# Score, solve and near copies in other shapes, constants inside the written order, and a new order, in a fused RWKV-7 and SwiGLU kernel

## The chip, the cores and the metric

The kernel runs on one core of a Trainium2 chip. The metric is the device time of one execution in microseconds; where several runs of a kernel are given, their median is compared.

## The reference

Two blocks follow each other. The first is the RWKV-7 recurrence over 768 steps for 4 x 8 heads of width 40; the second is a SwiGLU feed-forward block with RMS norm over 3072 tokens, 320 wide, with 1536 hidden units. All is float32.

```python
# r, k, v, w, a, b: (4, 8, 768, 40); state: (4, 8, 40, 40), zero at first
for t in range(S):
    y[:, :, t] = np.einsum('bhd,bhde->bhe', rt, state)
    Sa = np.einsum('bhde,bhe->bhd', state, at)
    state_decay = state * wt[:, :, None, :] - np.einsum('bhd,bhe->bhde', Sa, bt)
    state = state_decay + np.einsum('bhd,bhe->bhde', vt, kt)
x = y.transpose(0, 2, 1, 3).reshape(3072, 320)
xn = x / np.sqrt(np.mean(x * x, axis=-1, keepdims=True) + 1e-06) * rms_g
g = xn @ w_gate
out = (g * (1.0 / (1.0 + np.exp(-g))) * (xn @ w_val)) @ w_out
```

## The kernel before, in words

The sequence is cut into 24 chunks of 32 steps. Inside a chunk the recurrence becomes matrix products: a 32 x 32 triangular system per head is solved, and only the state passes from chunk to chunk. Batch and head give 32 sequences; they lie as 16 groups along the free axis (index n for 8 heads, o for two of the batches) and as four blocks of 32 partitions (i and q).

A chunk has three pieces of code. `front(c)` loads w, a, k, b and v, transposes them on TensorE (`turned`, line 527 in the profile), and builds by five levels (distances 1, 2, 4, 8, 16) the products of decayed k, b and a. The tile `LT` receives them: three predicated copies with the mask `near` (distances 1 to 3 inside groups of four steps) and one with `msk` for each higher level. `inverse(c)` takes the part of `LT` that belongs to b, sends it through DRAM (`sB`) into `M`, where each partition holds one sequence's matrix, eliminates row by row on VectorE (`Yi`, `tmp`), and sends the result through DRAM (`sY`) into the tile `LI`. While c is below `BLOCKED` (5) the elimination works on two 16 x 16 blocks, and `main` then solves twice with a correction by `LB` between. `main(c)` forms the right-hand side (the products called state and lower), multiplies it by the inverse (solve), updates the state, makes the scores of r against k and v (score), masks them by level (`As`, with `msi`), multiplies them with the level's k and b (level) and collects y. After the norm it writes the chunk, transposed, into `xg`.

`feed(g)` is the feed-forward block for a group of one or two chunks: products of `xg` with the resident weights `wf` into PSUM, silu on ScalarE (`sg`), product on VectorE (`hT`), and the product with w_out accumulated in `po`. `narrow(f, h, ...)` turns the weights, which arrive as 64-bit floats, into float32 on VectorE and ScalarE during the first chunks. The feed products wait for nothing but `xg`, `sg` and `hT`, and fill TensorE between the dependent steps of the chunks.

No scheduler decides the order at run time. Every operation is recorded by helpers as a piece of a `Plan`: `dve` (line 478, with `tt`, `ts`, `where` and `dcopy` above it), `act`, `copy` and `scale` for ScalarE (501, 505, 508), `ptt`, `pcopy` and `blank` for GpSimd (511, 514, 517), `dma` (521), and `pe` with `mm` (524) and `flip` (527). Therefore nearly all instructions carry one of these line numbers, and tiles tell them apart. `Plan.issue` then emits the pieces in the total order written in the table `ORDER`; `PAIRS` gives each PSUM use one of three double banks. Every engine and every DMA queue works through its own instructions in that order, so an instruction that waits holds up all behind it on its engine. SP issues most transfers, POOL (GpSimd's queue) the loads of w, a, k, b and v after the first chunk. `Turns(n, ...)` is a ring of n buffers; those with a `zero` view are cleared once by `blank`. The constants ahead of that (`ident`, `eye`, `msk`, `near`, `msi`) are issued directly, ahead of everything in the order.

The lines of the change in the kernel before, where the product of the score covers both batches i at once and the solve takes two 32 x 32 blocks as one block-diagonal 64 x 64 matrix:

```python
solve = [mm(U[half(i), o, col(m)], LI[half(i), 4 * o + m], Xs[half(i), o, col(m)])
         for m in range(4) for i in range(2) for o in range(2)]                      # 843
pe("score", [mm(sc[:, o, n], vut[part(o), n], R["rE"][part(o), n, :, tk])
             for n in range(N) for o in range(2)])                                   # 884
```

`half(i)` is the partitions 64i to 64i+63, `part(o)` the first 40 of a half, and `rows(i, x)` a block of 32.

Of the kernel before, what the change touches and what calls it, by code (L numbers as in the profile page):

```python
# [397 lines left out]
def kernel(  # L398
# [130 lines left out]
    def pe(kind, steps, more=[]):  # L529
        def issue(at):  # L530
            return [s[3](at) for s in steps]
        plan.add("PE", 0.0, 0.0, issue, [s[0] for s in steps] + more, [x for s in steps for x in s[1:3]],
                 kind=kind, many=sum(s[4] for s in steps))


    ident = const.tile([P, P], FP32, name="ident")
    nc.gpsimd.memset(ident, 0.0)
    nc.gpsimd.affine_select(ident, ident, pattern=[[-1, P]], channel_multiplier=1, base=0,
                            compare_op=ALU.not_equal, fill=1.0)
# [532 lines left out]
```

## Time and profile before

| | |
|---|---|
| median of 3 runs | 1184.49 us (1182.04 to 1191.2) |
| profiled execution, its time | 1190.31 us |
| its span, first to last instruction | 1188.5 us |
| TensorE busy, matmul | 1041.0 us (88%), 22896 records |
| TensorE busy, weight loads | 840.1 us (71%) |
| VectorE busy | 891.3 us (75%), 2917 instructions |
| ScalarE busy | 445.4 us (37%) |
| GpSimd busy | 304.6 us (26%) |
| mean granted TensorE clock | 0.929 |
| DMA traffic | 68.67 MB, mean 58 GB/s |

An fp32 product leaves two matmul records and two weight loads; a transpose leaves one of each. Matmuls overlap, so the mean time of one is a latency, and the busy time of a group divided by its count is what one occupies. Rows by shape read: line, engine, operation, output <- inputs, for a product weights K*M and then moving K x N, count, busy us, mean ns of one, then the engine's idle time just before and what ended it. PE is TensorE's matmuls, PEld its weight loads, DVE VectorE, ACT ScalarE, POOL GpSimd.

### The profile page before, as it was taken

Reading aid. Unit: us, or ns where it says so; the run is one execution under the profiler, and the core shown is the slowest. Engines: PE = TensorE matmul, PEld = TensorE weight load, DVE = VectorE, ACT = ScalarE, POOL = GpSimd, SP = SyncE. Lnnn points to the kernel's source line nnn. Section 1 sums busy time; section 2 is a strip of 40 time slices with the busy share of each in tenths; the row PEclk is TensorE's granted clock in tenths of the full one; section 3 lists DMA queues with packets and bytes.
Section 4 is the critical chain, followed back from the end, with each engine's and each line's share of the span. In section 5 each row is a group of like instructions: output and inputs, shape, how many; then the busy total and the mean of one; then the engine's idle time right before and its main releaser. Section 6 shows DMA issues by size and latency. Waiting matters only on the chain.

```text
span 1188.5 us, 52214 instructions
## 1 busy us (share of the span) xinstructions
PE 1041.0 (88%) x22896; PEld 840.1 (71%) x22896; DVE 891.3 (75%) x2917; ACT 445.4 (37%) x945; POOL 304.6 (26%) x534
## 2 busy tenths in 40 slices
PE   1528788998989899899899899999999999999998
PEld 1527777877877777777677777677777787777777
DVE  6999867669678777687787787797697686877541
ACT  4765552433242342433333433433324323413211
POOL 8203313223123232124124113124213132320000
PEclk9998667999998999998989999998899897999799
DMA  5464432231231231222223223222322222221110
GB/s 134 116 174 107 97 67 45 47 62 36 56 69 31 52 64 36 53 41 62 46 49 65 55 38 59 55 45 59 63 38 52 46 56 50 44 42 33 30 20 18
DMA packets 147043, 68.67 MB, mean 58 GB/s; under 512 B 121088, under 2 KB 136384, under 8 KB 146816
## 3 DMA queue, kind: packets, MB, share of 16 engines
q1 hardware_dynamic: 128448, 42.37, 16.0%
q0 software_dynamic: 16192, 22.64, 10.0%
q8 instruction: 180, 2.95, 1.0%
q10 hardware_dynamic: 2176, 0.33, 0.2%
q14 instruction: 47, 0.39, 0.1%
HBM read 55.05 MB, written 10.22 MB: 55 GB/s over the span
## 4 chain that ended last, share of the span: by engine, by line
PE 52%; DVE 28%; DMA 6%; issue 6%; SPq 3%; POOL 2%; ACT 2%; DVEq 0%; ACTq 0%; POOLq 0%
PE ps L524 39%; PE po L524 9%; DVE LT L478 7%; PE ps L527 4%; SPq L521 3%; DVE K L478 3%; DVE y L478 3%; DVE Yi L478 3%; DVE tmp L478 3%; DVE As L478 1%; DVE Ab L478 1%; DVE wf L478 1%; DMA sB<-LT 1%; DMA M<-sB 1%; POOL kbn L521 1%
## 5 line engine op out<-in xcount | busy, mean ns | idle before, releaser
L524 PE MATMUL ps<-xg,wf 64*128 64x256 f32 (+3 forms) x1872 | 391.8, 397 | 6.5 <-DVE LT L478 2.9
L524 PEld LDWEIGHTS ps<-xg,wf 64*128 64x128 f32 (+1 forms) x1872 | 281.7, 201 | 64.6 <-issue 20.7
L524 PE MATMUL po<-wf,hT 128*128 128x320 f32 x576 | 191.1, 465 | 0.6 <-DVE hT L478 0.6
L478 DVE TENSOR_TENSOR tmp<-Yi,M 128x60 f32<-128x60 f32 (+26 forms) x664 | 138.8, 209 | 38.9 <-ACT Yi L505 15.1
L478 DVE TENSOR_TENSOR Yi<-Yi,tmp 128x60 f32<-128x60 f32 (+26 forms) x664 | 138.0, 208 | 12.9
L524 PE MATMUL ps<-Ab,K 40*64 40x56 f32 x4608 | 101.8, 251 | 50.3 <-DVE K L478 12.8
L524 PEld LDWEIGHTS ps<-Ab,K 40*64 40x64 f32 x4608 | 93.3, 163 | 65.9 <-issue 33.5
L524 PEld LDWEIGHTS po<-wf,hT 128*128 128x128 f32 x576 | 106.9, 198 | 37.3 <-issue 3.8
L501 ACT ACTIVATE sg<-ps 128x256 f32<-128x256 f32 (+1 forms) x156 | 55.1, 368 | 173.1 <-PE ps L524 169.8
L478 DVE TENSOR_TENSOR hT<-ps,sg 128x256 f32<-128x256 f32 (+1 forms) x156 | 61.0, 401 | 65.9 <-PE ps L524 36.4
L478 DVE TENSOR_TENSOR As<-ps,msi 128x256 f32<-128x256 f32 (+1 forms) x192 | 85.9, 484 | 29.3 <-PE ps L524 29.3
L505 ACT COPY KN<-ps 128x640 f32<-128x640 f32 x96 | 66.0, 692 | 111.1 <-PE ps L527 49.1
L478 DVE TENSOR_TENSOR K<-K,T 128x512 f32<-128x512 f32 (+1 forms) x192 | 95.8, 511 | 3.4 <-PE ps L527 1.1
L521 POOL DMA_DIRECT2D wn<-in_w_dram x92 | 51.9, 567 | 177.2 <-DVE KN L478 128.1
L478 DVE COPY_PREDICATED LT<-near,ps 128x384 f32<-128x384 uint32 (+2 forms) x72 | 93.5, 1298 | 4.6 <-PE ps L524 4.1
L521 POOL DMA_DIRECT2D kbn<-in_b_dram x92 | 53.8, 587 | 165.6 <-PE ps L524 164.0
L521 POOL DMA_DIRECT2D kbn<-in_k_dram x92 | 53.7, 587 | 133.5 <-PE ps L524 127.9
L505 ACT COPY K<-K 128x512 f32<-128x512 f32 x96 | 60.9, 634 | 64.1 <-DVE K L478 33.7
L521 POOL DMA_DIRECT2D VU<-in_v_dram x92 | 53.8, 586 | 101.3 <-PE ps L524 98.7
L524 PE MATMUL ps<-As,KN 128*40 128x32 f32 x3072 | 74.9, 209 | 3.8 <-DVE As L478 2.5
L524 PEld LDWEIGHTS ps<-As,KN 128*40 128x40 f32 x3072 | 69.1, 130 | 11.2 <-DVE As L478 4.2
L511 POOL TENSOR_TENSOR ss<-ss,mhalf 128x1 f32<-128x1 f32 x24 | 14.8, 615 | 217.9 <-DVE ss L478 193.5
(131 smaller groups left out, 1507.1 us busy)
## 6 DMA issues: line engine op xcount, KB each, us to landing
M<-sB SPq DMA_DIRECT2D x96, 128.0 KB, 2.9
wan<-in_r_dram SPq DMA_DIRECT2D x24, 160.0 KB, 3.6
kbn<-in_b_dram POOLq DMA_DIRECT2D x92, 40.0 KB, 2.2
kbn<-in_k_dram POOLq DMA_DIRECT2D x92, 40.0 KB, 2.2
VU<-in_v_dram POOLq DMA_DIRECT2D x92, 40.0 KB, 2.6
wan<-in_w_dram POOLq DMA_DIRECT2D x46, 80.0 KB, 2.9
wan<-in_a_dram POOLq DMA_DIRECT2D x46, 80.0 KB, 2.8
wn<-in_w_dram POOLq DMA_DIRECT2D x92, 40.0 KB, 2.5
```

The lines of the kernel that those rows point to most:

```text
L478: plan.add("DVE", time + more + each * size(o), 0.087, lambda at: [fn(at(o), *m(at))], [o], aps(*args))
L501: scalar(o, [a], lambda at: nc.scalar.activation(at(o), at(a), f, **kw), aps(acc), 0.1 if f in (AF.Square, AF.Relu) else 0.0)
L505: scalar(o, [a], lambda at: nc.scalar.copy(at(o), at(a)), extra=more)
L511: plan.add("POOL", 0.5, 0.06, lambda at: nc.gpsimd.tensor_tensor(o, a, b, op), [o], [a, b])
L521: plan.add(by, 0.6 if by == "POOL" else 0.45, 0.0, lambda at: queue.dma_start(out=o, in_=i), [o], [i], load=load, since=since)
L524: return o, lhsT, rhs, lambda at: nc.tensor.matmul(at(o), lhsT, rhs, start=start, stop=stop, skip_group_check=True), 4
L527: return o, i, ident, lambda at: nc.tensor.transpose(at(o), i, ident), 2
```

## The change

- Score: two products of 64 x 32 take the place of each of 128 x 64, one for each i. The score masks read the one 32-column block twice by a broadcast.
- Solve: two products of 32 x 32 for each of 64 x 64. The tile `LI` goes; the inverse is written into the block of `LT` that it came from, and the products run in the order of the lower products.
- Near copies: the elements are visited with the steps inside a group of four innermost.
- While c is below 5, the two copies into `r2` and the second half of the copies into `VU` move from VectorE to ScalarE.
- `kbn` has three buffers instead of two.
- The constants are recorded as pieces and stand in the total order; the first buffers of `wan`, `kbn`, `wn`, `A` and `VU` are cleared by VectorE.
- `ORDER` and `PAIRS` are new throughout, made by a planner whose model lets waits hold up TensorE's instruction blocks.

```diff
-    iw[...] = ...   # constants: nc.vector.* and nc.gpsimd.* issued directly
+    iota(iw[:, 0], [[0, C]], 1)          # recorded pieces: blank, select, iota, ts, tt, pcopy
+    ts(iw[:, 0], iw[:, 0], C - 1, None, ALU.bitwise_and)
...
+    EARLY = "wan", "kbn", "wn", "A", "VU"
...
             for i, t in enumerate(self.tiles if zero else []):
-                blank(zero(t), fill)
+                if i == 0 and name in EARLY:
+                    dve(0.065, nc.vector.memset, zero(t), fill)
+                else:
+                    blank(zero(t), fill)
...
-    kbn = Turns(2, [P, N, 2, 64], "kbn", pad)
+    kbn = Turns(3, [P, N, 2, 64], "kbn", pad)
-    LI_ = Turns(2, [P, N, 2 * C], "LI", whole)
...
-            where(LT.rearrange("p n (g j) -> p j n g", j=4)[:, dist:], near[:, dist - 1].rearrange(
-                "p (g j) -> p j g", j=4)[:, dist:, None].bitcast(U32).to_broadcast((P, m, NI, 8)),
-                g4.rearrange("p n g j -> p j n g")[:, at:at + m])
+            where(LT.rearrange("p n (g j) -> p n g j", j=4)[:, :, :, dist:], near[:, dist - 1:dist].rearrange(
+                "p u (g j) -> p u g j", j=4)[:, :, :, dist:].bitcast(U32).to_broadcast((P, NI, 8, m)), g4[:, :, :, at:at + m], more=0.12)
...
-            dma(LI[rows(i, 1 - q), :, (1 - q) * C:(2 - q) * C], sY[seq(i, q)].rearrange("m (s t) -> s m t", s=C), "LT")
+            dma(LT[rows(i, 1 - q), q::2], sY[seq(i, q)].rearrange("m (s t) -> s m t", s=C), "LT")
...
-        solve = [mm(U[half(i), o, col(m)], LI[half(i), 4 * o + m], Xs[half(i), o, col(m)]) for m in range(4) for i in range(2) for o in range(2)]
-        pe("solve", solve)
+        solve = [mm(U[other(i, n), o, col(n % 4)], LT[other(i, n), o * N + slot(n)], Xs[other(i, n), o, col(n % 4)])
+                 for n, i, o in by_q]
+        pe("lower", solve)
...
-            (copy, dcopy)[q](VU[other(i, 4 * q), 4 * q:4 * q + 4, :, 0:D].rearrange("p n o d -> p o n d"),
+            (copy, copy if c < BLOCKED else dcopy)[q](VU[other(i, 4 * q), 4 * q:4 * q + 4, :, 0:D].rearrange("p n o d -> p o n d"),
...
-            dcopy(R["r2"][half(0)], ps[half(1), :, 0])
-            dcopy(R["r2"][half(1)], ps[half(0), :, 1])
+            cross = copy if c < BLOCKED else dcopy
+            cross(R["r2"][half(0)], ps[half(1), :, 0])
+            cross(R["r2"][half(1)], ps[half(0), :, 1])
...
-        pe("score", [mm(sc[:, o, n], vut[part(o), n], R["rE"][part(o), n, :, tk]) for n in range(N) for o in range(2)])
-        si = sc.rearrange("p o n (i t) -> p (o n) i t", i=2)
+        pe("score", [mm(sc[half(i), o, n, 0:C], vut[part(o), n, half(i)], R["rE"][part(o), n, i, tk])
+                          for n, i, o in each])
...
-                tt(As[:, j], si[:, :, :, 1 if l == 1 else 16:C:2 if l == 1 else 1],
+                tt(As[:, j], sc.rearrange("p o n t -> p (o n) t")[:, :, None, 1 if l == 1 else 16:C:2 if l == 1 else 1].to_broadcast((P, NI, 2, 16)),
```

More of the change, by code (lines that the diff above doesn't have):

```diff
@@ L33 @@
 ORDER = """
[194 rows of a table removed]
[199 rows of a table added]
 """
 PAIRS = """
-01201122220202101122021002120010112120200010121011221110122101022120221112022201002110110012121201220201000020002102
-02012222221022111110111121012101101221211010020020202001222202000102012122101200002011201110022012202012220200101010
-22101221210220122211102101120120010200212010121121200121110222122020221002021001120122200212101101102011220201100011
-01022200200100101122022212011110122111211121222021222000112101000102020010121120020101110102110002202111112002100102
-002212220202010101112102021201201
+01201012220202101120011021120120120001211101200220022011212212002010211202010111202220002221212201002020112222100202
+11120010020202000102011001010121120210201020221221211022220202210010102221111201110101220020120112120222210212002121
+22022202001020202101122000210022020100000210111211020121212111212101112102020121001001202020102012121212221200012210
+12101101020220202022121021222220201102201012000121201021120222202000022102011100020122001111110121202010202002222000
+102002120102200100221221212101210
 """
@@ L533, in pe, with pool, select, iota @@
                  kind=kind, many=sum(s[4] for s in steps))
+    def pool(time, o, fn, ins=()):
+        plan.add("POOL", time, 0.06, lambda at: fn(), [o], list(ins))
+    def select(o, pattern, base, mult):
+        pool(0.23 + 0.0008 * size(o), o, lambda: nc.gpsimd.affine_select(
+            o, o, pattern=pattern, channel_multiplier=mult, base=base, compare_op=ALU.not_equal, fill=1.0), [o])
+    def iota(o, pattern, mult):
+        pool(0.1, o, lambda: nc.gpsimd.iota(o, pattern=pattern, base=0, channel_multiplier=mult))
     ident = const.tile([P, P], FP32, name="ident")
-    nc.gpsimd.memset(ident, 0.0)
-    nc.gpsimd.affine_select(ident, ident, pattern=[[-1, P]], channel_multiplier=1, base=0,
-                            compare_op=ALU.not_equal, fill=1.0)
+    blank(ident, 0.0)
+    select(ident, [[-1, P]], 0, 1)
     po_ = psum.tile([P, 2, 512], FP32, name="po")
@@ L548 @@
     iw = eye[:, 0:3].bitcast(I32)
-    nc.gpsimd.iota(iw[:, 0], pattern=[[0, C]], base=0, channel_multiplier=1)
-    nc.gpsimd.iota(iw[:, 1], pattern=[[1, C]], base=0, channel_multiplier=0)
-    nc.vector.tensor_scalar(iw[:, 0], iw[:, 0], C - 1, None, ALU.bitwise_and)
-    nc.vector.tensor_tensor(iw[:, 0], iw[:, 0], iw[:, 1], ALU.bitwise_xor)
+    iota(iw[:, 0], [[0, C]], 1)
+    iota(iw[:, 1], [[1, C]], 0)
+    ts(iw[:, 0], iw[:, 0], C - 1, None, ALU.bitwise_and)
+    tt(iw[:, 0], iw[:, 0], iw[:, 1], ALU.bitwise_xor)
     msk = const.tile([P, len(LEVELS), C], FP32, name="msk")
     for j, l in enumerate(LEVELS):
-        nc.vector.tensor_scalar(iw[:, 2], iw[:, 0], j, None, ALU.logical_shift_right)
-        nc.vector.tensor_scalar(msk[:, j], iw[:, 2], 1.0, None, ALU.is_equal)
+        ts(iw[:, 2], iw[:, 0], j, None, ALU.logical_shift_right)
+        ts(msk[:, j], iw[:, 2], 1.0, None, ALU.is_equal)
     near = const.tile([P, 3, C], FP32, name="near")
     same = const.tile([P, C], FP32, name="same")
-    nc.vector.tensor_scalar(same, iw[:, 0], 4.0, None, ALU.is_lt)
-    nc.vector.tensor_tensor(iw[:, 2], iw[:, 0], iw[:, 1], ALU.bitwise_xor)
-    nc.vector.tensor_tensor(iw[:, 2], iw[:, 1], iw[:, 2], SUB)
+    ts(same, iw[:, 0], 4.0, None, ALU.is_lt)
+    tt(iw[:, 2], iw[:, 0], iw[:, 1], ALU.bitwise_xor)
+    tt(iw[:, 2], iw[:, 1], iw[:, 2], SUB)
     for dist in range(3):
-        nc.vector.tensor_scalar(near[:, dist], iw[:, 2], float(dist + 1), None, ALU.is_equal)
-        nc.vector.tensor_tensor(near[:, dist], near[:, dist], same, MUL)
+        ts(near[:, dist], iw[:, 2], float(dist + 1), None, ALU.is_equal)
+        tt(near[:, dist], near[:, dist], same, MUL)
     msi = const.tile([P, len(LEVELS), 2, 16], FP32, name="msi")
-    nc.gpsimd.memset(msi, 0.0)
+    blank(msi, 0.0)
     for j, l in enumerate(LEVELS):
         for i in range(2):
-            nc.gpsimd.tensor_copy(msi[half(i), j, i:i + 1].rearrange("p n (g l) -> p n g l", l=l), side(msk[half(i)], l, 1)[:, j:j + 1])
+            pcopy(msi[half(i), j, i:i + 1].rearrange("p n (g l) -> p n g l", l=l), side(msk[half(i)], l, 1)[:, j:j + 1])
     mhalf = const.tile([P, 1], FP32, name="mhalf")
-    nc.gpsimd.memset(mhalf, -0.5)
+    blank(mhalf, -0.5)
     c1151, c255 = const.tile([P, 1], FP32, name="c1151"), const.tile([P, 1], FP32, name="c255")
@@ L579 @@
         dma(gcol[p0:p0 + m, kt:kt + 1], moe_rms_g[src:src + m].rearrange("(d o) -> d o", o=1), "g")
-    nc.gpsimd.memset(eye, 0.0)
+    blank(eye, 0.0)
     for m in range(4):
         e = eye[m * BH:(m + 1) * BH]
-        nc.gpsimd.affine_select(e, e, pattern=[[-4, C // 4], [1, C]], channel_multiplier=0, base=-m,
-                                compare_op=ALU.not_equal, fill=1.0)
+        select(e, [[-4, C // 4], [1, C]], -m, 0)
+    EARLY = "wan", "kbn", "wn", "A", "VU"
     class Turns:
@@ L796, in inverse @@
         plan.stage = "inverse", c
-        M, LI = z["M"], LI_.next()
-        z["LI"] = LI
+        M, LT = z["M"], z["LT"]
         Yt = Yi_.next()
@@ L841, in main @@
         U = plan.room()
-        LI = z["LI"]
-        solve = [mm(U[half(i), o, col(m)], LI[half(i), 4 * o + m], Xs[half(i), o, col(m)]) for m in range(4) for i in range(2) for o in range(2)]
-        pe("solve", solve)
+        solve = [mm(U[other(i, n), o, col(n % 4)], LT[other(i, n), o * N + slot(n)], Xs[other(i, n), o, col(n % 4)])
+                 for n, i, o in by_q]
+        pe("lower", solve)
         if c < BLOCKED:
@@ L851, in main @@
             scale(Xs, X[:, :, 0:4 * D], -1.0)
-            pe("solve", solve)
+            pe("lower", solve)
         for i, q in each_iq:
-            (copy, dcopy)[q](VU[other(i, 4 * q), 4 * q:4 * q + 4, :, 0:D].rearrange("p n o d -> p o n d"),
+            (copy, copy if c < BLOCKED else dcopy)[q](VU[other(i, 4 * q), 4 * q:4 * q + 4, :, 0:D].rearrange("p n o d -> p o n d"),
                              U[other(i, 4 * q), :, 0:4 * D].rearrange("p o (n d) -> p o n d", n=4), more=0.09)
@@ L893, in main @@
                 for i in range(2):
-                    tt(As[:, j, :, i].rearrange("p n (g l) -> p n g l", g=G), side(si[:, :, i], l, 1),
+                    tt(As[:, j, :, i].rearrange("p n (g l) -> p n g l", g=G),
+                       side(sc.rearrange("p o n t -> p (o n) t")[:, :, 0:C], l, 1),
                        msi[:, j:j + 1, i].rearrange("p n (g l) -> p n g l", g=G).to_broadcast((P, NI, G, l)), MUL)
```

393 rows, old and new, of the table ORDER are left out of this document.

## The prediction

> **What bounds the kernel now.** I read the page's head, the busy slices and the chain first, then cut the span where TensorE's first feed product starts, then the groups by shape and the waits.
>
> ```profile
> span 1188.5 us, 52214 instructions
> PE   1528788998989899899899899999999999999998
> DVE  6999867669678777687787787797697686877541
> PEclk9998667999998999998989999998899897999799
> PE 52%; DVE 28%; DMA 6%; issue 6%; SPq 3%; POOL 2%; ACT 2%; DVEq 0%; ACTq 0%; POOLq 0%
> ```
>
> Slices are 29.7 us wide. In the first five VectorE (DVE) is the busier engine and TensorE (PE) has gaps; from the sixth on PE stands at 8 or 9. The chain that ended last agrees: PE 52%, VectorE 28%. The two stretches need separate sums, and the border is the first product of the feed, which is all the filler that PE has:
>
> ```profile
> 154.76 1.73 PE L524 MATMUL ps<-xg,wf 64*128 64x128 f32 x9
> 0.00:151.00 151.00, 78.75 (x2262) 71.82 (x2262) 133.37 (x362) 86.60 (x158) 55.55 (x112) 0.88 0.51 124
> 151.00:1188.50 1037.50, 962.25 (x20634) 768.29 (x20634) 757.93 (x2556) 358.80 (x787) 249.06 (x423) 0.94 0.24 48
> ```
>
> The columns are stretch, length, then busy PE, PEld, DVE, ACT, POOL, granted clock, DMA share, GB/s. Up to 151 us VectorE is busy 133.4 of 151, PE 78.8. After it PE is busy 962.3 of 1037.5 (92.7%) and VectorE 73%. So the start lasts as long as VectorE's queue ahead of the first feed product, and the rest lasts PE's work divided by 0.927; a microsecond less of PE work there is worth 1.08 us at the end if the share of idle time stays.
>
> **The score and solve products** (PE groups, first all, then those after 151 us):
>
> ```profile
> L524 PE MATMUL ps<-rE,vut 40*128 40x64 f32 x768 | 54.0, 295 | 2.1 <-ACT vut L505 1.3 <-issue 0.7
> L524 PE MATMUL ps<-Xs,LI 64*64 64x40 f32 x928 | 38.8, 238 | 18.0 <-DMA LI<-sY 12.6 <-issue 2.5 <-ACT Xs L508 2.1
> L524 PE MATMUL ps<-rE,vut 40*128 40x64 f32 x704 | 46.7, 284 | 1.0 <-issue 0.7 <-ACT vut L505 0.2
> L524 PE MATMUL ps<-Xs,LI 64*64 64x40 f32 x800 | 31.7, 230 | 6.5 <-DMA LI<-sY 2.5 <-issue 2.5 <-ACT Xs L508 0.7
> L524 PE MATMUL ps<-Ab,K 40*64 40x56 f32 x4032 | 84.1, 242 | 39.1 <-DVE K L478 8.2 <-DVE Yi L478 6.7 <-DVE Ab L478 6.5
> L524 PE MATMUL ps<-VU,KN 64*40 64x40 f32 x1408 | 21.0, 219 | 0.8 <-ACT KN L505 0.5 <-issue 0.3
> L524 PE MATMUL ps<-VU,LT 32*32 32x40 f32 x1344 | 17.6, 199 | 5.1 <-issue 5.1
> L524 PE MATMUL ps<-ST,aP 40*32 40x40 f32 x1344 | 17.1, 204 | 0.2 <-DVE ST L478 0.2
> L524 PE MATMUL ps<-Xs,LB 16*32 16x40 f32 x192 | 2.9, 220 | 0.0
> L524 PE MATMUL ps<-As,KN 128*40 128x32 f32 x3072 | 74.9, 209 | 3.8 <-DVE As L478 2.5 <-DVE tmp L478 0.8 <-issue 0.5
> ```
>
> Each fp32 product leaves two records. The mean ns of one is its latency; what a group occupies is busy time over count, since neighbours in different quadrants of the array overlap. A score group is 32 records; after 151 us there are 704/32 = 22 of them at 46.7/22 = 2.12 us. The new score has 64 records, each with 64 weight columns and 32 moving columns, cycling over the four quadrants as Ab,K does. Ab,K has the same weights but 56 moving columns: 84.1/63 = 1.33 us per 64 records, the upper bound. ST,aP, the quickest 64-record row, gives 17.1/21 = 0.81, the lower bound. VU,KN (40 moving columns, all four quadrants) gives 21.0/22 = 0.95. I take 0.95: 22 x (0.95 - 2.12) = -26 us, bounds -17 to -29.
>
> A solve group is 32 records at 31.7/25 = 1.27 us (25 after 151 us, since a blocked chunk solves twice). The new one is a VU,LT group in shape and count, 32x32 weights and 40 columns: 17.6/21 = 0.84. So 25 x (0.84 - 1.27) = -11 us, bounds 0.97 (Xs,LB: 2.9/3) for -7 and 0.81 for -11.5.
>
> Together -36 of PE's 962 (-25 to -40), times 1.08 is **-39 us** (-27 to -43). Before 151 us the same edit saves some 5 us of PE work, hidden by VectorE's queue; without that cover it would be 5 more.
>
> The Trainium skill (TensorE: Matmul & The Clock Gate, "Wait — 56ns, not 53.3ns?") says that starts never come closer than about 25 ns however few the columns, and its page TensorEngine Tiling (Array Packing), "Instruction Overhead", advises against splitting a dimension that is already small. By 25 ns a record a group of 64 would take 1.6 us: the solve would be slower than now, and the two edits together would save 3 us of PE work after 151 us instead of 36. The VU,LT row has 17.6 us for 1344 records, 13 ns each, so for products that change quadrant the trace disagrees; the third rival below is what is left of it.
>
> **The near copies** (VectorE, by shape):
>
> ```profile
> L478 DVE COPY_PREDICATED LT<-near,ps 128x384 f32<-128x384 uint32 x24 | 45.2, 1882 | 4.2 <-PE ps L524 4.1
> L478 DVE COPY_PREDICATED LT<-near,ps 128x256 f32<-128x256 uint32 x24 | 31.0, 1293 | 0.2
> L478 DVE COPY_PREDICATED LT<-near,ps 128x128 f32<-128x128 uint32 x24 | 17.3, 719 | 0.2
> L478 DVE COPY_PREDICATED LT<-msk,ps 128x256 f32<-128x256 uint32 x72 | 31.1, 432 | 32.2 <-PE ps L524 25.1 <-ACT KN L505 6.7
> L478 DVE TENSOR_TENSOR A<-A,T 128x256 f32<-128x256 f32 x24 | 10.8, 452 | 4.7 <-ACT A L505 4.3 <-ACT T L505 0.3
> L478 DVE TENSOR_TENSOR T<-T 128x256 f32<-128x256 f32 x24 | 10.0, 418 | 0.6 <-ACT T L505 0.6
> L478 DVE TENSOR_TENSOR T<-T 128x128 f32<-128x128 f32 x24 | 6.9, 288 | 0.0
> ```
>
> The same instruction on 256 elements takes 432 ns with the level masks, whose elements lie in runs, and 1293 ns with the near mask, whose innermost step jumps 16 bytes in LT and mask and 28 in PSUM. Three near copies cost 1.88 + 1.29 + 0.72 = 3.89 us a chunk. The change puts the three, two or one neighbours innermost. From the T rows an element costs 1.02 ns and an instruction 157 ns, so 384 would take 0.55 in long runs; runs of two add 34 ns (A<-A,T against T<-T). I take 0.60 + 0.45, and 0.72 unchanged for the third, whose run is one element: 1.77 us, **-2.1 us a chunk**, 51 us of VectorE in all. Bounds: nothing, if the price belongs to something else than the step, and -2.6 if the third falls too; a loss is excluded by those 34 ns. After 151 us VectorE is not the bound, so this pays only through what PE waits for:
>
> ```profile
> PE ps L524 <- issue: 14.6, 16, 1.7
> PE ps L524 <- DVE LT L478: 9.3, 4, 2.9
> PE ps L524 <- DVE K L478: 8.2, 6, 2.8
> PE ps L524 <- DVE Ab L478: 6.5, 4, 2.2
> PE ps L524 <- DVE T L478: 2.1, 1, 2.1
> ```
>
> (engine waiting, releaser, us in total, times, longest; after 151 us). LT, K, Ab and T are VectorE's steps of the front around the copies: 26 us of PE's 75 idle. I take a third, **-9 us** (0 to -26); what is late next in those places is the K scaling. The first row is PE waiting for no semaphore, inside dense groups of small products. The change adds 1696 product records and as many weight loads, 3392 on 52214; I take **+3 us** (0 to +15).
>
> **The start.** The constants are now steps of the order, and five first buffers are cleared on VectorE; copies of r2 and half of VU go to ScalarE while c < 5.
>
> ```profile
> ACT A L505 <- POOL A L517: 4.5, 1, 4.5
> L478 DVE COPY r<-ps 64x512 f32<-64x512 f32 x24 | 16.5, 689 | 14.9 <-ACT rE L505 7.1 <-PE ps L527 4.1 <-ACT Xs L508 3.3
> L478 DVE COPY VU<-ps 32x320 f32<-32x320 f32 x48 | 23.2, 484 | 36.6 <-PE ps L524 36.0
> ```
>
> ScalarE waited 4.5 us for GpSimd to clear A, and VectorE stood behind it: -4.5. The five clears are about 3 us of VectorE, in a gap before its first loads land. The r2 and VU copies are 0.69 and 0.48 us each; ScalarE is busy 87 of 151 us and takes them under that cover, but if ScalarE's copies out of PSUM queue up there they would cost the same back. The new order matters more. In the built programs the first feed product stands behind 11 Ab,K groups and 3 lower groups now, behind 15 and 4 afterwards: one chunk more is sent ahead. VectorE's queue up to the instruction that PE last waits for there grows by 96 instructions, at 891.3/2917 = 0.306 us (busy and count of the whole run) 29 us; less four near sets at 2.1 and the 4.5: about +16. The 96 hold more full-width instructions (0.42 us) than narrow ones (0.2 us), so I take **+20**, between 0 (if PE meets its inputs as early as now) and +29: first feed product at 175 us.
>
> **Other parts.** A third kbn buffer frees loads that waited for PE; PE's own waits for kbn loads are under 3 us, so I count nothing, and the early loads keep their cover of a chunk. LI is gone: the inverse is sent into LT's own block, by four transfers of the size they had, and front c+2 must wait for the solve of chunk c instead of its lower products, a microsecond or so of PE work later. In the built order at least 33 VectorE instructions, 10 us at 0.306, stand between the first score mask of c, which is behind the solve, and that front's first copy into LT; without them that microsecond a chunk is the price. Score masks read the same number of elements.
>
> **The sum,** against the profiled span of 1188.5. PE's work before the first feed product is 82 us now; one chunk more without feed is about 18 and the smaller groups there save 5: 95. PE's total is 1041 - 42 = 999 (whole-run rows: score 54.0 to 24 x 0.96, solve 38.8 to 29 x 0.88, is -44; I keep -42). Then 175 + (999 - 95)/0.927 = 175 + 975 = 1150; -9 and +3 give 1144 us. The profiled execution took 1190.31 us, 1.8 outside the span, while the runs' median is 1184.49; scaled by 1184.49/1188.5 the forecast is **1140 us**.
>
> **The rivals.**
> 1. *PE's idle share falls as well* (to 4%), because VectorE is lighter and the order fits: 175 + 904/0.96 + 3 = 1120, scaled 1116. For it: most waits after 151 us are for VectorE. Against: the order is new everywhere. 0.10.
> 2. *The near copies keep their price.* Then 8.5 us come back in the start and 9 after it: 1158. For it: the msk rows also differ in mask and operand layout. 0.10.
> 3. *Small products run at the pace of the level row,* 74.9/3072 = 24.4 ns, as if a floor per record: score 1536 x 0.0244 = 37.5 instead of 54.0, solve 1856 x 0.0244 = 45.3 instead of 38.8, net -10: 26 x 1.08 more than the forecast, 1168. Against: VU,LT and ST,aP. 0.08.
> 4. *Slower: the solve waits.* It stands behind four transfers from sY at the end of the inverse's chain, and feed products queue behind it on PE. Now such waits are 12.6 us in all. If each of some 21 chunks waited 2.7 us more, PE's idle time would go from 71 to 128 us and the time past 1196. Against: between the end of an inverse and its chunk's first score mask the new order keeps at least 35 VectorE instructions and the old one 33, but for the last chunk. 0.06.
> 5. *The order gives it back:* filler that starts 20 us later and waits in other places bring it to within 1%, with all instructions as cheap as forecast. 0.04.
>
> **How the numbers follow.** The forecast has 0.62. About 1% is what a measurement of this kernel can tell from no change, so faster means below 1172.6. Forecast, rivals 1 and 2 and a part of 3 lie there; I take 0.02 off for the forecast's upper end: 0.83. Rival 5, most of 3 and that end give 0.09, rival 4 with a tail 0.08. The range: low by rival 1 and the full price on the waits, 1106; high past rival 3, 1176.
>
> **What would show it.** Right: score and solve groups under 1.1 and 1.0 us; near copies under 0.8, 0.6 and 0.75; first feed product between 165 and 185 us; PE busy about 1000 us and 92 to 94% of the rest. Wrong: near copies over 1 us, 64-record groups at 1.5 us, or PE busy under 90% after the first feed product.

## The result, and the profile after

Four runs of the changed kernel took 1101.64 us in the median (1093.9 to 1104.41), four of the kernel before on the same chip 1183.26 us: a ratio of 0.9288, 95% interval 0.9222 to 0.9353, or 82 us less. The forecast was 1140 us, 43 less, in a range from 1106 to 1176: the sign is right, and the time is 4.4 us below the range. The profiled execution took 1093.9 us, the fastest of the four; the profiled one of before, 1190.31 us, lies above its median, so the two traces are 96.5 us apart where the medians differ by 82.

The head of the page after, its slices for TensorE and the granted clock, and the chain that ended last:

```profile
span 1092.0 us, 55580 instructions
PE 974.0 (89%) x24592; PEld 782.8 (72%) x24592; DVE 840.1 (77%) x2906; ACT 448.7 (41%) x961; POOL 302.3 (28%) x528
PE   2647578999999889999999999899999999999998
PEclk9996656899999999999999999999999999999999
PE 55%; DVE 18%; DMA 8%; SPq 7%; issue 6%; ACT 3%; POOL 2%; DVEq 0%; ACTq 0%; POOLq 0%
```

From the ninth slice on the clock stands at 9 throughout; before, 7s and 8s lay all along the kernel. In the chain VectorE went from 28% to 18%. The first feed product, by the timeline after:

```profile
193.47 1.20 PE L529 MATMUL ps<-xg,wf 64*128 64x128 f32 x8
```

It starts 39 us later than before (154.76), 18 later than forecast. The stretches on its two sides, in the windows view (columns as in the prediction):

```profile
0.00:193.50 193.50, 118.29 (x4054) 107.23 (x4054) 165.96 (x479) 116.48 (x221) 75.63 (x142) 0.77 0.50 117
193.50:1092.00 898.50, 855.76 (x20544) 675.57 (x20542) 674.13 (x2428) 332.19 (x740) 226.63 (x386) 0.99 0.26 52
```

TensorE is busy 95.2% of the second stretch, at a clock of 0.99; before it was 92.7% at 0.94. The 0.77 of the start is too high: the view counts time without a clock record as full, and the first record stands at 83.7 us here and at 101.4 before. Ahead of 83.7 us an Ab,K record, of unchanged shape, lasts 312 ns in the mean of both traces, as do the 576 in the trace after that lie under half clock; behind 200 us, near full clock, they last 220 there. So both kernels begin at half clock, for longer than the rows say.

The groups by shape after:

```profile
L529 PE MATMUL ps<-rE,vut 40*64 40x32 f32 x1536 | 30.5, 232 | 0.9 <-ACT vut L510 0.4 <-issue 0.2
L529 PE MATMUL ps<-Xs,LT 32*32 32x40 f32 x1856 | 28.6, 214 | 23.6 <-DMA LT<-sY 15.5 <-ACT A L510 3.6 <-ACT Xs L513 2.4
L483 DVE COPY_PREDICATED LT<-near,ps 128x384 f32<-128x384 uint32 x24 | 17.5, 727 | 3.5 <-PE ps L529 2.1 <-ACT x L513 1.0 <-issue 0.2
L483 DVE COPY_PREDICATED LT<-near,ps 128x256 f32<-128x256 uint32 x24 | 17.4, 724 | 0.1
L483 DVE COPY_PREDICATED LT<-near,ps 128x128 f32<-128x128 uint32 x24 | 17.5, 730 | 0.2
L529 PE MATMUL ps<-xg,wf 128*128 128x256 f32 x1056 | 264.8, 391 | 0.5 <-issue 0.3
L529 PE MATMUL po<-wf,hT 128*128 128x320 f32 x576 | 183.4, 448 | 0.2
```

Two of these groups are the same work as before, and yet shorter. Before they read:

```profile
L524 PE MATMUL ps<-xg,wf 128*128 128x256 f32 x1056 | 275.5, 404 | 1.3 <-ACT sg L501 1.3
L524 PE MATMUL po<-wf,hT 128*128 128x320 f32 x576 | 191.1, 465 | 0.6 <-DVE hT L478 0.6
```

The change leaves these products as they were, and together they lost 18 us. What differs is the clock at which they ran, 0.94 and 0.99 in the windows. TensorE's waits after the first feed product, after the change (as in the prediction: total, times, longest):

```profile
PE ps L529 <- issue: 15.9, 18, 2.1
PE ps L529 <- DMA LT<-sY: 3.8, 5, 1.8
PE ps L532 <- issue: 2.4, 4, 1.6
...
PE ps L532 <- DVE LT L483: 1.2, 1, 1.2
```

The waits for the front's VectorE steps, 26 us before, are all but gone: 1.2 us for LT is the largest of them.

**What the clock does in the kernel before.** Windows of the trace before, around two gaps in TensorE's work (the column after POOL is the granted clock):

```profile
814.80:818.20 3.40, 1.89 (x98) 1.36 (x96) 3.30 (x13) 0.00 (x0) 0.00 (x0) 0.99 0.00 0
818.20:825.00 6.80, 6.28 (x121) 5.17 (x117) 5.64 (x24) 1.33 (x4) 0.56 (x1) 0.50 0.01 2
825.00:828.40 3.40, 3.40 (x66) 2.84 (x63) 2.54 (x11) 1.26 (x4) 3.02 (x6) 1.00 0.23 41
1094.70:1098.10 3.40, 1.45 (x20) 0.76 (x19) 3.40 (x7) 0.01 (x1) 0.00 (x0) 0.99 0.00 0
1098.10:1111.70 13.60, 13.60 (x285) 10.77 (x284) 4.34 (x14) 5.21 (x11) 1.70 (x3) 0.50 0.13 24
1111.70:1115.00 3.30, 3.30 (x16) 2.91 (x17) 2.24 (x3) 0.38 (x1) 0.00 (x0) 1.00 0.51 159
```

A stretch of 3.4 us in which TensorE was busy for 1.9 or 1.5 us is followed by 6.8 and 13.6 us at half clock, although TensorE works through nearly all of them; VectorE, busy 3.3 and 3.4 us, was what it had waited for. The same product costs twice as much there. The po products in the groups of 1098.1 to 1111.7 us, and of 1111.7 to 1125 us:

```profile
L524 PE MATMUL po<-wf,hT 128*128 128x320 f32 x4 | 2.5, 781 | 0.0
L524 PE MATMUL po<-wf,hT 128*128 128x320 f32 x9 | 2.7, 432 | 0.0
```

A product occupies 2.5/4 = 0.63 us in the first and 2.7/9 = 0.30 us in the second.

In all sixteen traces that have clock records, the stretches at half clock behind 200 us last a whole number of 3.41 us, one to four, but for those that the end cuts. Cut into such windows, from 200 us to 20 us before the end, they show what a window at full clock is followed by. With TensorE busy for less than 40% of it, half clock came in 31 of 31 cases; at 40 to 50% in 35 of 38, at 50 to 60% in 28 of 57, at 60 to 70% in 28 of 124, and above that in 17 of 3808. The way back is harder: of the windows at half clock in which TensorE was busy for 95% or more, 142 of 188 were the last, of the less busy ones 1 of 22.

The Trainium skill (TensorE: Matmul & The Clock Gate, "Part 1: The HAM clock gate") describes this: activity is judged in windows of some 3.4 us, and the clock is either full or half. The traces agree: their records hold 0.5 and 1.0 alone, and 3.41 us is the unit. The page's section "HAM oscillation — how this bites in real kernels" puts the danger at gaps of over 3.4 us; here waits of 1.5 and 1.7 us were enough.

### The profile page after: what moved, and what is told of

It is laid out like the page before. It is cut to its first block, busy times and chain, and to the rows that moved or that the text cites. A ratio compares the mean times of both kernels' runs of the same rounds, so it can differ in the third digit from the quotient of the medians.

```text
span 1092.0 us, 55580 instructions
## 1 busy us (share of the span) xinstructions
PE 974.0 (89%) x24592; PEld 782.8 (72%) x24592; DVE 840.1 (77%) x2906; ACT 448.7 (41%) x961; POOL 302.3 (28%) x528
## 4 chain that ended last, share of the span: by engine, by line
PE 55%; DVE 18%; DMA 8%; SPq 7%; issue 6%; ACT 3%; POOL 2%; DVEq 0%; ACTq 0%; POOLq 0%
PE ps L529 41%; PE po L529 10%; SPq L526 7%; PE ps L532 5%; DVE tmp L483 3%; DVE Yi L483 3%; DMA M<-sB 2%; DVE As L483 2%; DVE y L483 2%; DMA LT<-sY 2%; DMA sB<-LT 2%; DVE LT L483 1%; DVE wf L483 1%; DVE exs L483 1%; DVE K L483 1%
## 5 line engine op out<-in xcount | busy, mean ns | idle before, releaser
L529 PE MATMUL ps<-xg,wf 128*128 128x256 f32 (+3 forms) x1872 | 370.5, 380 | 3.3 <-DVE hT L483 1.7
L529 PEld LDWEIGHTS ps<-xg,wf 128*128 128x128 f32 (+1 forms) x1872 | 268.6, 192 | 57.6 <-issue 17.1
L529 PE MATMUL po<-wf,hT 128*128 128x320 f32 x576 | 183.4, 448 | 0.2
L529 PEld LDWEIGHTS po<-wf,hT 128*128 128x128 f32 x576 | 103.0, 190 | 34.8 <-DVE hT L483 1.6
L529 PE MATMUL ps<-Ab,K 40*64 40x56 f32 x4608 | 93.7, 239 | 16.2 <-DVE K L483 4.5
L529 PEld LDWEIGHTS ps<-Ab,K 40*64 40x64 f32 x4608 | 85.6, 153 | 29.3 <-issue 14.4
L483 DVE TENSOR_TENSOR K<-K,T 128x512 f32<-128x512 f32 (+1 forms) x192 | 93.5, 497 | 3.2 <-ACT K L510 1.2
L483 DVE TENSOR_TENSOR As<-ps,msi 128x256 f32<-128x256 f32 (+1 forms) x192 | 88.1, 482 | 5.6 <-PE ps L529 5.2
L483 DVE COPY_PREDICATED LT<-near,ps 128x384 f32<-128x384 uint32 (+2 forms) x72 | 52.3, 727 | 3.8 <-PE ps L529 2.1
```

Of the source, the lines that this page charges most:

```text
L483: plan.add("DVE", time + more + each * size(o), 0.087, lambda at: [fn(at(o), *m(at))], [o], aps(*args))
L529: return o, lhsT, rhs, lambda at: nc.tensor.matmul(at(o), lhsT, rhs, start=start, stop=stop, skip_group_check=True), 4
```

## The experiments

Theory 1 is the prediction's: a wait of TensorE costs its own length and a product its own duration. Theory 2: a gap that leaves TensorE idle for a good part of a window also halves its clock for one or more windows after it, and half of that time is lost.

To tell them apart, the traces are cut at 200 us, behind which TensorE is the bound in every kernel here. Idle is the sum of the gaps between its products; half is the time that the clock's records stand at 0.5, both up to the last product; work is the length less idle less half of half, so what the products would take at full clock, with the 4 to 5 us behind the last product. Each row is one execution.

| after 200 us, in us | length | idle | half | work |
|---|---|---|---|---|
| before | 988.5 | 69.1 | 105.8 | 866.5 |
| b_near2 | 931.5 | 42.1 | 47.8 | 865.5 |
| b_score | 947.1 | 65.2 | 71.7 | 846.0 |
| b_solve | 984.0 | 65.8 | 129.1 | 853.7 |
| b_all | 900.3 | 44.9 | 30.7 | 840.0 |
| after | 892.0 | 38.1 | 6.8 | 850.5 |
| a_oldnear | 934.1 | 57.6 | 43.8 | 854.6 |
| a_oldscore | 923.7 | 40.1 | 41.0 | 863.1 |
| a_oldboth | 948.1 | 58.3 | 44.6 | 867.5 |
| b_fill | 964.1 | 34.3 | 47.8 | 905.9 |
| b_fill2 | 957.3 | 50.5 | 23.9 | 894.9 |
| b_all3 | 895.4 | 34.6 | 10.2 | 855.7 |

From before to after the length falls by 96.5: 31 idle, 49.5 clock (99 us less at half), 16 work. Half-clock time differs between executions of one kernel, but the mean clock of every execution tells the same. The span times one less the mean clock is the time that a whole run lost to the clock, as far as it was recorded: on average 83 us in 34 executions of before, 54 in b_near2, 41 in b_near, 45 in b_fill2 and 43 in b_all. After has 57, since it has 95.6 us at half clock up to 200 us where before has 61.4.

**Near copies alone** (b_near, and b_near2 for its trace):

```diff
-where(LT.rearrange("p n (g j) -> p j n g", j=4)[:, dist:], ...)
+where(LT.rearrange("p n (g j) -> p n g j", j=4)[:, :, :, dist:], ...)
```

> The kernel before with one change: the near copies write runs of consecutive elements (128, 96 of... all with 128 runs per copy), nothing else; order, score and solve are the old ones. The three copies should fall to about 0.73 us each (2.18 us a chunk instead of 3.89), and with that the first feed product comes about 5 to 8 us earlier. Theory 1 (the prediction's: a wait of TensorE costs its own length): the start gains 7 us and the waits after 200 us that end at the near copies some 9 us more: about 1167 us. Theory 2 (the clock: each gap of about 2 us that the near copies leave in TensorE's work lets the granted clock fall to half for 3.4 to 13.7 us after it): the half-clock time after 200 us falls from 105 us to under 40, each us of it gives back half a us, so some 30 us come on top of the 16: about 1135 us (1120 to 1150).

> Again the kernel before with the near copies in the new shape alone, for its trace. The first time it took 1112 to 1121 us at a mean clock of 0.960 to 0.966 (before: 1181 at 0.932), 61 us less, more than both theories gave. Theory 2 with both terms larger: the trace shows TensorE's idle time after 200 us down by 20 us or more from 69.1 us, and its half-clock time after 200 us down from 105.8 us to 15 to 35 us. If theory 2 is wrong, the half-clock time has stayed over 80 us, or the time came out of work that got shorter for another reason.

Measured: 1119.12 us in the median of three executions of b_near (ratio 0.947, 0.9395 to 0.9545) and 1133.47 us in b_near2 (0.9531, 0.9458 to 0.9603), some 55 to 63 us less. A fourth execution of b_near, the profiled one, took 2294.03 us and left no clock record; its trace is not used. No product changed, and the work column says so: 866.5 and 865.5. All of it is idle time (27) and clock (29). Idle fell as expected; the half-clock time fell by 58 us but, at 47.8, stayed above the expected 15 to 35. The first feed product came at 152.2 us, 2.6 earlier and not 5 to 8. The stretch and TensorE's waits in it for the front's VectorE steps, after 152 us, in the trace of b_near2:

```profile
200.00:1131.50 931.50, 884.81 (x19452) 704.70 (x19448) 683.80 (x2433) 334.06 (x736) 232.38 (x396) 0.97 0.25 50
```

```profile
PE ps L524 <- DVE LT L478: 2.8, 3, 1.4
PE ps L524 <- DVE K L478: 1.8, 4, 0.6
PE ps L524 <- DVE Ab L478: 1.0, 2, 0.5
PE ps L524 <- DVE T L478: 0.6, 1, 0.6
```

The 26 us became 6, and none is longer than 1.4 us, where they reached 2.9. Theory 1 is refuted as a full account: it gave 1167.

**Score alone, solve alone, all three in the old order** (b_score, b_solve, b_all):

```diff
-pe("score", [mm(sc[:, o, n], vut[part(o), n], R["rE"][part(o), n, :, tk]) ...
+pe("score", [mm(sc[half(i), o, n, 0:C], vut[part(o), n, half(i)], R["rE"][part(o), n, i, tk]) ...
-solve = [mm(U[half(i), o, col(m)], LI[half(i), 4 * o + m], Xs[half(i), o, col(m)]) ...
+solve = [mm(U[other(i, n), o, col(n % 4)], LT[other(i, n), o * N + slot(n)], Xs[...]) ...
```

> The kernel before with one change: the score products are split into halves (32 rows by 32 columns from 64), nothing else. The after trace shows 1.27 us a group of 24 us less in sum, with records near 20 ns. Theory 1 and theory 2 expect the same: 24 us less PE work, 1158 to 1162 us; under theory 2 the half-clock time after 200 us stays near 100 us, because the near copies and the gaps that they leave stay.

> The kernel before with one change: the solve is split and the inverse goes into LT, nothing else (the copy of the old inverse tile stays allocated, unused). The groups measured in the after trace give 10 us less PE work: 1172 to 1175 us in both theories. Rival 4 of the prediction: the solve then waits for the transfer into LT, which the near copies of the next chunk's LT also hold up: 1185 us or more, with a PE wait LT<-sY over 15 us.

> The kernel before with the three parts together (split score, split solve, new near copies), in the old order and with the constants issued as before. Theory 1: 1183 less 24, 10 and 16 is about 1133 us, and the missing 31 us to the kernel after must be the work of the new order. Theory 2: the parts alone bring the half-clock time after 200 us under 40 us and the time to 1100 to 1115 us; the new order and the constants then are worth less than 10 us.

b_score took 1159.83 us in the median, in the range that both theories gave, but by luck, since no execution lies there: its four runs came in pairs, 1146.2 and 1148.9 us at clocks of 0.945 and 0.944, 1170.8 and 1173.4 at 0.928 and 0.926: the same program, 25 us apart, with the span times the clock between 1081 and 1085 in all four. The trace is of the 1148.9; its work fell by 20, and its half-clock time to 71.7 us, where theory 2 had near 100. b_solve took 1176.2 us, ratio 0.9983 (0.9946 to 1.002), so no gain is shown in time; its trace, of the slowest of ten executions, has 13 us less work and 23 more at half clock. TensorE's wait LT<-sY is 6.4 us after 200 us there, not the 15 of the fourth rival. b_all took 1100.54 us, 0.9327 (0.9272 to 0.9381): with the old order and the old constants it is level with the kernel after. Theory 2 holds for it (30.7 us at half clock, under 40), theory 1's 1133 doesn't.

**The parts undone in the kernel after** (the diffs above reversed):

> The kernel after with one part undone: the near copies write the old shape (3.89 us a chunk). Theory 1 (a wait costs its own length): about 16 us more than after, 1115 to 1120 us. Theory 2 (gaps cost clock): windows at half clock return after 200 us, 60 us of them or more where the kernel after has 7, and the time rises by 30 to 50 us, to 1130 to 1150 us.

> The kernel after with one part undone: the score products are the old, whole ones. Both theories: 23 us more PE work, 1122 to 1127 us, and no half-clock windows come back after 200 us.

> The kernel after with the old near copies and the old score; new are the order, the constants' issue and the solve. If the new order is worth something by itself (the missing 31 us under theory 1) this stands at 1140 to 1150 us, 33 to 43 under the kernel before. If it is worth nothing and theory 2 holds, at 1165 to 1178 us: the kernel before less the 10 us of the solve, give or take the clock.

a_oldnear: 1133.12 us (0.9611, 0.9554 to 0.9668), 32 above after, as theory 2 said, though with 44 us of half clock where 60 were expected; idle and clock share the difference, 19.5 and 18.5. Its stretch, and that of after:

```profile
200.00:1134.10 934.10, 871.91 (x20540) 684.45 (x20538) 705.45 (x2428) 332.65 (x740) 226.69 (x386) 0.98 0.25 50
```

```profile
200.00:1092.00 892.00, 849.32 (x20484) 669.84 (x20482) 672.12 (x2422) 328.95 (x733) 226.03 (x385) 1.00 0.26 51
```

a_oldscore: 1121.12 us, 19 above after, a little under what was expected; that no half clock would come back was wrong (41.0 us). a_oldboth: 1149.28 us (0.9755, 0.970 to 0.9811). It differs from b_solve by the order, the constants, the buffers that came with them and the copies moved to ScalarE, and stands 27 us below it: half-clock time 129.1 against 44.6 in the traces, idle 65.8 against 58.3, work 14 more. With the old near copies the new order and what came with it are worth those 27 us, mostly through the clock; with the new ones (b_all against after) nothing that can be told apart. So the two seem to mend the same gaps.

**Gaps filled, no wait removed** (b_fill, b_fill2). Dummy products into a part of a PSUM bank that nobody reads stand ahead of waits in the kernel before:

```diff
+    for _ in range(FILL.get(self.done, 0) if p.engine == "PE" else 0):
+        self.warm()      # nc.tensor.matmul(po_[:, 0, DM:DM + P], ident, ident, ...)
```

> The kernel before with nothing taken away; dummy products of 128x128 that write a scratch bank which nobody reads stand ahead of 45 of TensorE's waits after 200 us (waits over 0.5 us, 60 us in all), sized to fill some 85 percent of each. Theory 1: the waits stay as long, and what does not fit into them is added: 1183 to 1195 us. Theory 2: TensorE is busy through the gaps, the clock stays full in most of the 105 us that ran at half after 200 us, and the time falls by 25 to 45 us, to 1138 to 1158 us, though not one wait is removed.

> The kernel before with 120 dummy products (some 28 us) ahead of the 29 waits of TensorE after 200 us that were over 1 us (48.5 us together), each filled to 60 percent; a wait inside a group has its dummies ahead of the group. In the first such kernel the dummies added 39 us of work, fell short of some places, and took the idle time down by 35 us and the half-clock time by 58 us (29 us of time). Theory 2: with less surplus work the clock's part stays: half-clock time after 200 us under 60 us, and 1145 to 1162 us, 20 to 35 us below the kernel before, though TensorE does more work and waits for the same things. Theory 1: the dummies only replace waiting, 1178 to 1190 us.

b_fill: 1165.31 us, 0.9895 (0.983 to 0.9959), in neither theory's range. The half-clock time fell by 58 us, but the dummies, 179 of which the trace shows, added 39 us of work. b_fill2, with 120 for the long gaps alone: 1159.14 us, 0.9782 (0.9655 to 0.9908) of the kernel before, which took 1191.1 us on that chip: a gain of about 2%, in theory 2's range and below theory 1's. Its stretch, and the one before:

```profile
200.00:1157.30 957.30, 902.28 (x19670) 725.48 (x19662) 715.76 (x2433) 334.14 (x736) 232.79 (x396) 0.99 0.24 49
```

```profile
200.00:1188.50 988.50, 914.89 (x19546) 727.88 (x19540) 723.91 (x2450) 338.30 (x743) 233.06 (x396) 0.95 0.24 47
```

TensorE executes 240 product records more in all, VectorE's near copies are the old ones, and yet TensorE's busy time falls by 12.6 us (in the stretch, and in all from 1041.0 to 1028.4), since the clock rises from 0.95 to 0.99. This shows theory 2's mechanism apart from the copies; what it is worth in time, when the gaps stay, is small.

**Filling what is left** (b_alllate, b_all2, b_all3 in the old order with all three parts; b_allfill with the start too; a_fill for the start of after):

> The kernel with all three parts in the old order, and 51 dummy products (some 11 us) ahead of those 14 of TensorE's waits after 200 us that were over 1 us in its trace; each wait is filled to 60 percent. That kernel had 30.7 us at half clock after 200 us and took 1100.5 us. Theory 2: under 10 us at half clock remain there and the time falls by 5 to 12 us, to 1088 to 1095 us. Theory 1: no gain, or up to 5 us more.

> The kernel with all three parts in the old order, with 47 dummy products (some 11 us) ahead of the 14 waits after 200 us over 1 us, none left out this time (before, only 22 of 51 found their place). Theory 2: half-clock time after 200 us from 30.7 us to under 12, idle time from 45 to some 36 us: 1086 to 1096 us, under the kernel after. Theory 1, or dummies that only move the gaps: 1098 to 1108 us.

> As the one before, with 65 dummy products ahead of 23 waits over 0.7 us (25.8 us). Theory 2: the same half-clock time as with 14 waits, under 12 us, and 1085 to 1097 us; the shorter waits do not pull the clock down, so their dummies bring nothing more. If new gaps arise where the dummies push the work, half-clock time stays at 20 to 40 us and the time at 1098 to 1108 us.

> As the one with dummy products late, and also ahead of 21 waits over 0.4 us between 60 and 200 us, where the kernel with all three parts stood at half clock for 54.6 us. Theory 2, if TensorE's chain helps to set the start: 30 us or more of that half clock go, and 5 to 15 us more of the time than with the late ones alone. If VectorE's queue alone sets the first feed product, the start stays as long, within 3 us, at a full clock.

> The kernel after with 118 dummy products (26 us) ahead of 28 of TensorE's waits between 60 and 192 us (31.6 us of waits); it stood at half clock there for 95.6 us. If TensorE's chain at half clock sets the start, the first feed product comes 10 us or more ahead of 193 us and the time falls to 1080 to 1095 us; if VectorE's queue or the transfers set it, the time stays at 1095 to 1105 us, or the dummies that do not fit delay it by up to 10 us.

None beats the kernel after beyond doubt. b_alllate (1106.85 us) says nothing: only 22 of its dummies found their places, and the half-clock time stayed at 30.7 us. b_all2 took 1103.35 us at 15.2 us of half clock, b_all3 1098.97 us (0.9283, 0.9208 to 0.9358) at 10.2 us: the clock came back, the added work took it away again, and the forecast gains of 5 us and more did not come. b_allfill, 150 of whose 188 dummies the trace shows: 1107.09 us, with 41.0 us of half clock left in the first 200 where b_all has 54.6, so 14 less and not the 30. a_fill, 106 of whose 118 dummies it shows: 1102.07, 1107.96 and 1115.99 us, and 1349.11 us in a fourth execution, at a clock of 0.665. Its first feed product, in the list of its line:

```profile
L535 PE MATMUL ps<-xg,wf x206: 272/275/771, 190.2 to 259.9; 128*128 128x128 f32 x48, 64*128 64x128 f32 x24, 128*128 128x256 f32 x19, 64*128 64x256 f32 x12
```

With 54.6 us of recorded half clock in the first 200 us instead of 95.6 it starts at 190.2 instead of 193.5 us, and behind 200 us the trace has 38.8 us at half clock where the kernel after has 6.8. How much the half clock of the start costs is not shown by this, since the dummies take time there too. Nor does VectorE's queue alone set the start of the kernel after: in the chain that ended last it leads up to 140 us; then come the transfers that carry the inverse into LT, until 151.7, and from there to the first feed product 63% of the chain are TensorE's own products.

## Why the prediction was right in sign and half in size

The sum gave 1144 us of span, the trace 1092 (8 of the 52 because it is of the fastest of four executions). With the measured values in its own form: the start +18.5 (193.5 for 175); TensorE's work after it 855.8 instead of 904, -48.2/0.927 = -52; its idle share 4.8% instead of 7.3%, 923.2 to 898.5, -25; the separate terms for waits and issue, now contained in that share, +6. Together 1092.

- **The step that failed** is "the rest lasts PE's work divided by 0.927". It takes busy time as a property of the products and idle time as a share that follows it. The prediction quoted the clock row with its 7s and 8s and gave it no term. Of the 48 us that the work was short, 23 were only done earlier (118.3 instead of 95 us ahead of the feed); the other 25 are TensorE's total of 974 instead of 999. The groups that nobody changed, xg and po, fell by 18 in the two rows above alone: the clock. In the cut at 200 us the clock is 49.5 of 96.5 us.
- **The price of the waits** was the second mis-sized term: "a third, -9". b_near2 shows 27 us less idle time, about the whole 26 that the rows had, and as much again from the clock behind the gaps. The upper bound fits the idle time, and the choice of a third was a guess without a row. "What is late next" (the K scaling) took nothing back worth naming: 1.8 us.
- **Score** was put at -26 after 151 us (2.12 to 0.95 a group); measured are 30.5/24 = 1.27 a group, near the Ab,K bound of 1.33, and 20 us of work. VU,KN was not the nearest row. **Solve**: 28.6/29 = 0.99 instead of 0.84, at the bound of 0.97; 13 us of work against -11, and no gain in time by itself. Of the limits that were given, 1.1 and 1.0 us a group, only the solve kept its own.
- **Near copies**: 2.18 us a chunk instead of 1.77, since all three cost 0.73. The third was left as it was, the other two did not fall to the price of long runs.
- **Start**: 193.5 us, later than its own range, which ended at 184. The forecast let VectorE's queue set it; the chain shows the inverse's transfers and TensorE's own products behind 140 us. Yet it was harmless: b_all, whose first feed product came at 149.6 us, took as long. The price of a late feed is what TensorE can't do meanwhile, and it did 23 us of other work.
- **Issue**: 15.9 us on the row that had 14.6, and 2.4 on the one of the transposes, which had 0.4 before: +3 came true in sum, over stretches of unequal length.
- **Rivals.** The first (idle share to 4%, 1116) described best what came, at a chance of 0.10, and still lacked the clock. The second fell with the near rows, the third with 30.5/1536 = 19.9 and 28.6/1856 = 15.4 ns a record: under the 24.4 ns of the level row, on which it rested. The fourth found no such wait where it mattered: LT<-sY is 3.8 us after the first feed product and 11.8 ahead of it, 15.5 in all against 12.6 for LI<-sY. The fifth is half true: the order brings nothing of its own in time once the near copies are short, but takes nothing either.

Open: what of the 27 us (with the old copies) is the order and what the constants, the third kbn buffer, the early clears or the copies moved to ScalarE; these were not taken apart. Open too is what a start at full clock would be worth.

## What to carry to other kernels

Where the row of the granted clock shows anything below full speed in a stretch that TensorE bounds, a gap in its work can have two prices, its length and half of the slow time behind it; look for the gap ahead of each slow window and price both. Gains that mend the same gaps do not add up: shorter copies were worth some 55 to 63 us, and a new order with what came with it 27, each without the other, and the order nothing more once the copies were short. Useless products that keep the clock up were worth little here, 2% in the kernel before and nothing that could be measured once the copies were short, since they take time themselves; shorten what makes TensorE wait.

## What the hardware showed that was not expected

- A wait of 1.5 to 1.7 us, with TensorE busy 1.9 or 1.5 of 3.4 us, was followed by 6.8 and 13.6 us at half clock. In the 34 executions of the kernel before that ran beside the experiments, on four chips, the time ranged from 1165.2 us (clock 0.945) to 1196.0 (0.919), with a correlation of -0.88 between time and clock: over three quarters of the variance of one program go with the clock.
- A predicated copy into LT took 0.73 us whether it wrote three, two or one of the four elements of each of 128 groups, and 1.88, 1.29 and 0.72 us when its 384, 256 or 128 elements are each visited apart: (1882 - 719)/256 = 4.5 ns for each visit to a group. A group is four floats, 16 bytes. The Trainium skill (SBUF — State Buffer, "Door 1: The DMA port swizzle") speaks of lines of 16 bytes and a penalty for each access that changes the line; the rows agree with such a penalty. Whether it lies in LT, in the mask or in PSUM, all of which the copy steps through, they do not tell.
- Neighbouring products in different quadrants ran at 15.4 and 19.9 ns a record, small as they are.
